# One constant's loads on GpSimd's queue, the identity on the sync queue, and a new order of work

## The chip, the cores and the metric

The kernel runs on one core of one Trainium2 chip. A core has five engines that run their own instruction streams side by side: PE (matrix products; its weight loads are listed apart as PEld), DVE (VectorE), ACT (ScalarE), POOL (GpSimd) and SP (SyncE, which does nothing here but issue transfers). Transfers between DRAM and the core's on-chip memory (SBUF) are moved by 16 DMA engines; each is issued by an instruction of some engine, and an engine issues its transfers in the order in which they stand in its stream. The metric is the device time of one execution in microseconds (us); the median of the runs is compared.

## The reference

Two paths read the same layernormed input and are added to it. Shapes: 2048 tokens, 512 channels, 128 states for each channel, 1792 hidden units; all inputs are bf16.

```python
xn = layernorm(x)                              # over the 512 channels
out = x + A(xn) + B(xn)

# B: gated linear unit
h = sigmoid(xn @ w_gate) * (xn @ w_up)
B = h @ w_down

# A: state-space convolution
logdA = exp(log_dt)[:, None] * (A_re + 1j * A_im)
P = exp(logdA[:, :, None] * arange(2048))                       # 512 x 128 x 2048
K = einsum("dn,dnl,dn->dl", C, P, exp(log_dt)[:, None] * B).real  # 512 x 2048
A = causal_convolution_along_tokens(xn, K) + xn * Dskip         # by FFT of 4096
```

## The kernel before

**The two paths.** The layernorm comes first: four x tiles of 128 tokens by 512 channels are loaded one by one, the others in larger pieces; DVE makes the statistics (L537) and the normalised tiles (L549), and PE transposes the first tiles with an identity matrix (L559, `ident`). Path B then runs in four groups of 512 tokens: gate products (L1042), up products (L1067), ACT's sigmoid (L1055) and copy (L1082), DVE's product of the two (L1087) and the down-projection (L1119). The sum of input and down-projection is made by an accumulating transfer that POOL issues (L1156), 256 KB for two token tiles, in the first three groups.

Path A replaces the long convolution by a transform along the tokens, cut into two steps. The transformed input goes through a DRAM scratch `z_scr`. The convolution kernel K comes from tables of powers that DVE and ACT build (L660 to L740, L789), and PE sums over the states (L820); it goes through a DRAM scratch `k_scr`. Then come 16 *units*: the channels are cut into two halves (p = 0 and 1, of 256 channels), and in each half eight units u = 0 to 7 stand for groups of frequencies. A unit is this chain:

- its input is loaded from `z_scr` (256 KB, on SP), transformed by PE (L881, eight matmuls) and copied to SBUF (ACT, or DVE where `ON_DVE` says so);
- a second copy of it with its halves swapped is made, by four 64 KB transfers on SP (L889) in the first half and for units 4, 6, 7 of the second, and by four DVE copies (L894) for the other five units of the second half;
- its piece of the constant E (`c_E`, 320 KB) is loaded into one of the three slots of the pool `es`, and PE makes the unit's kernel transform from it (L907, ten matmuls);
- DVE multiplies the two (L912, L916), PE transforms back (L931, two matmul shapes), the result is copied and stored to a DRAM scratch `v_scr`.

At the end `v_scr` is read back, and the last PE products (`final`, L1017) add it to what path B left.

**E and its slots.** A slot of `es` is freed by the L907 that reads it. The pieces of units 4, 6 and 7 stay in their slots from the first half to the second (`SHARED`), so there are 8 + 5 = 13 loads; in the second half the loads of units 5, 3, 2, 0 and 1 each wait for a slot that an L907 of this half frees. In the second half the load of unit 5 takes the slot that unit 7's L907 frees, and those of units 0 and 1 the slots of units 5 and 3.

**What sets the order.** `_Plan.add` only records an operation with its engine, its dependences and the slots that it takes and frees. `run` then walks through `ORDER`, a list of all operation numbers, and gives each operation to its engine and each slot to the next taker in that sequence. So `ORDER` sets the stream of every engine, SP's and POOL's too: a transfer whose data or slot isn't there yet holds up all that stands behind it on its engine.

In the lines below, L430 is where every transfer of the helper `dma` is issued (so the profile puts all of them on L430), with the engine as the first argument:

```python
dma("SP", es, cten["E"].ap()[u], deps=w_use[0], acq=[esl], ...)(320 * KB)      # L899
o_held = pl.add("ACT", 0.2, lambda: S.activation(out=ident[:, 127:128], in_=one[:], ...))
l_id = load("ACT", ident[:], cten["ident"].ap(), 32 * KB, deps=[o_held])
```

Before, the identity's transfer is on ACT's queue, behind `o_held`, a small ACT write into a column of `ident`.

Tensors in the profile that are called `big` lie in one large SBUF buffer, so most rows of path A read `big<-big`; `pair` and `bank` are PSUM buffers of 1024 and 512 columns.

Of the kernel before, what the change touches and what calls it, by code (L numbers as in the profile page):

```python
# [13 lines left out]
ACT = mybir.ActivationFunctionType  # L14
# [55 lines left out]
KB = 1024  # L70
# [114 lines left out]
def _consts():  # L185
# [18 lines left out]
                MAB=f(MAB), E=f(_build_E(M2, by).reshape(128, NU // 2, 2, NKT, 128).transpose(1, 0, 2, 3, 4)))  # L204

UEV = (6, 7, 10, 11, 12, 13, 14, 15, 16, 17, 18, 19, 22, 23, 24, 25, 26, 27, 28, 29, 30, 31, 32, 33, 34, 35, 36, 37, 38, 39, 40, 41, 44, 45, 46, 47, 52, 53, 54, 55,)
ON_DVE = (84, 87, 102, 104, 119, 120, 121, 135, 136, 182, 193, 194, 196, 197, 199, 229, 276, 286, 334, 338, 362, 431, 495,)
ORDER = [
# [41 lines left out]

class _Op:
    __slots__ = ("alt", "tab", "eng", "cost", "fn", "prio", "acq", "rel", "dma", "left", "users", "ready", "start", "done", "seq", "mode")
# [69 lines left out]
def kernel(  # L322
# [12 lines left out]
    V, S, T, P, Y = nc.vector, nc.scalar, nc.tensor, nc.gpsimd, nc.sync  # L335
    QUEUE = {"SP": Y, "ACT": S, "POOL": P}
    cten = {k: nc.inline_tensor(v, name="c_" + k) for k, v in _consts().items()}
# [6 lines left out]
    pl = _Plan(dict(s=NS, gu=NGU, hT=NHT, zs=4, zx=2, xx=3, es=3, kb=2, pp=2, pq=2, vs=2, ot=5, tg=2, us=2, sq=2))  # L344
# [14 lines left out]
    ident = const.tile([128, 128], BF, name="ident")  # L359
# [62 lines left out]
    def dma(q, dst, src, deps=(), prio=0.0, acq=(), rel=(), pkt=1024, after=None, hv=0.5):  # L422

        n = None
        get = lambda v: v() if callable(v) else v
        holder = {}

        def fn():
            with nc.allow_non_contiguous_dma(reason="laid out"):
                holder["i"] = QUEUE[q].dma_start(out=get(dst), in_=get(src))  # L430
            if after:
                after(holder["i"])

        return lambda nbytes: pl.add(q, 0.62, fn, deps, prio, acq, rel, dma=(nbytes, _rate(pkt), hv))
# [4 lines left out]
    def load(q, dst, src, nbytes, deps=(), pkt=2048, hv=0.5):  # L439
        lp[0] += 0.01  # L440
        return dma(q, dst, src, deps=deps, prio=lp[0], pkt=pkt, hv=hv)(nbytes)
# [14 lines left out]
    one = const.tile([128, 1], F32, name="one")  # L456
    P.memset(one[:], 1.0)
    S.add_instruction(mybir.InstLoadActFuncSet(name=nc.get_next_instruction_name(), act_func_set_id=LN_EXP_SET))
    o_held = pl.add("ACT", 0.2, lambda: S.activation(out=ident[:, 127:128], in_=one[:], func=ACT.Identity), (), 0)
    l_pa = load("SP", par[:, 0:3, :], A_par[:, 0:3, :], 384 * KB, pkt=3072)  # L460
    l_id = load("ACT", ident[:], cten["ident"].ap(), 32 * KB, deps=[o_held])
    l_pbc = load("SP", par[:, 3:7, :], A_par[:, 3:7, :], 512 * KB, pkt=4096)
    wgv = B_w_gate.rearrange("(kt p) f -> p kt f", p=128)
    wuv = B_w_up.rearrange("(kt p) f -> p kt f", p=128)
# [137 lines left out]
    for n in ["t1", "t2"]:  # L602
# [3 lines left out]
                                                   func=ACT.Exp), [l_pa], 5, tab="exp")  # L606
# [113 lines left out]
    w_use, g_use = [[], []], [[], []]  # L720
# [25 lines left out]
    for c in range(4):  # L746
# [64 lines left out]
        for half_ in range(2):  # L811
            sl = _Slot("s")

            def f_k(half_=half_, sl=sl, G=G, H=H):
                for y in range(8 * half_, 8 * half_ + 8):
                    pk = bank(sl, y // 4 % 2).rearrange("p (q x) -> p q x", q=4)
                    for comp in range(2):
# [18 lines left out]
                        deps=kq_free + W_op + [o_g], prio=PC, pkt=384)(192 * KB))  # L836
# [29 lines left out]
    for p in range(NP):  # L866
        dsl = slice(DW * p, DW * p + DW)
        for u in UNITS[p]:
# [27 lines left out]
            if p and u in SHARED:  # L896
                esl, es, le = held_e[u]
            else:
                le = dma("SP", es, cten["E"].ap()[u], deps=w_use[0], prio=QP - 0.5, acq=[esl], pkt=2560, hv=0.9)(320 * KB)  # L899
                held_e[u] = esl, es, le  # L900
            sk = _Slot("s")

# [306 lines left out]
```

## Time and profile before

| | |
|---|---|
| median of 3 runs | 214.41 us (213.24 to 215.0) |
| the profiled execution: its time, its span | 215.62 us, 213.8 us |
| granted TensorE clock, mean | 0.996 |
| instructions in the span | 4897 |
| moved by DMA | 42.07 MB, 197 GB/s in the mean |
| accumulating transfers on POOL (q0) | 1.57 MB, 5.1% of the 16 engines' span |

How to read what the prediction shows of the profile: the span is the time from the first to the last instruction of one execution; the execution's own time has a little around it. Busy shares are of the span. The slices cut the span in 40 equal parts of 5.34 us, a digit for each: the busy share in tenths. In rows of groups, `xN` is the number of instructions, and the number after the bar the busy time and the mean of one in ns. In rows of the timeline the first number is the start in us, the second the duration of the row, and the brackets give the idle time just ahead and what ended it. A wait `A <- B` stands for idle time of A that B's end finished, as total, count and longest. SPq is the sync queue's own issuing.

### The profile page before, as it was taken

To read this page: it belongs to the slowest core of one execution; us is meant where nothing else is said; L and a number is where in the kernel's file an instruction comes from. 1 tells how busy PE (TensorE), PEld (TensorE's weight loads), DVE (VectorE), ACT (ScalarE), POOL (GpSimd) and SP (SyncE) were. 2 spreads that over 40 slices of the span, in tenths; PEclk is the share of its full clock that TensorE was granted. 3 is DMA by queue.
4 is the path that set the end of the run, shared out by engine and by line. 5 is a ranking of instruction groups with operands and counts; after the bars stand their busy time and mean duration, and the time that the engine had idled before them with its cause. 6 is when DMAs were issued, how large, how long until landed. Compare 5 with 4: busy or idle time off the path is not lost.

```text
span 213.8 us, 4897 instructions
## 1 busy us (share of the span) xinstructions
PE 204.4 (96%) x1856; PEld 102.4 (48%) x1856; DVE 195.5 (91%) x412; ACT 171.5 (80%) x274; POOL 16.8 (8%) x30
## 2 busy tenths in 40 slices
PE   7898999999999999999999999999999979999992
PEld 2653444444444454445437464544653636644571
DVE  3889999999999999999999999999997979994583
ACT  3599999999999999988799998877968777891000
POOL 1003006200820000110000000011000000000000
PEclk9999999999999999999999999999999999999998
DMA  5999379101791457897575778787585569989644
GB/s 169 310 395 364 126 171 311 55 6 38 244 165 46 147 167 249 202 208 189 115 219 143 218 208 251 196 237 156 126 224 161 145 188 321 312 236 296 213 172 172
DMA packets 51465, 42.07 MB, mean 197 GB/s; under 512 B 16545, under 2 KB 44978, under 8 KB 51250
## 3 DMA queue, kind: packets, MB, share of 16 engines
q1 hardware_dynamic: 49650, 39.72, 61.7%
q0 software_dynamic: 864, 1.57, 5.1%
q10 hardware_dynamic: 928, 0.47, 0.8%
q8 instruction: 14, 0.23, 0.4%
q14 instruction: 9, 0.07, 0.1%
HBM read 24.44 MB, written 12.85 MB: 174 GB/s over the span
## 4 chain that ended last, share of the span: by engine, by line
DVE 61%; PE 20%; DMA 6%; ACT 5%; issue 4%; SPq 1%; DVEq 0%; ACTq 0%
DVE big L735 10%; DVE big L734 10%; DVE big L740 5%; DVE big L739 5%; PE bank L1119 4%; DVE hT_sb L1087 4%; PE bank L1042 4%; PE pair L931 3%; DVE big L673 3%; DVE big L675 3%; DVE big L912 3%; PE pair L907 3%; DVE hT_sb L1092 3%; PE bank L1067 3%; DVE stats L537 2%
## 5 line engine op out<-in xcount | busy, mean ns | idle before, releaser
L291 ACT ACTIVATE big<-pair 128x1024 bf16<-128x1024 f32 x62 | 64.3, 1065 | 9.1 <-PE pair L881 1.7
L1067 PE MATMUL bank<-xnT,wu_sb 128*128 128x512 bf16 x224 | 53.6, 379 | 0.1
L1119 PE MATMUL bank<-wd_sb,hT_sb 128*128 128x512 bf16 (+1 forms) x238 | 50.4, 367 | 0.0
L1042 PE MATMUL bank<-xnT,wg_sb 128*128 128x512 bf16 (+1 forms) x200 | 46.8, 371 | 1.0 <-ACT hT_sb L1055 0.9
L1042 PEld LDWEIGHTS <-wg_sb 128*128 128x128 bf16 x240 | 22.4, 98 | 26.1 <-issue 4.7
L1119 PEld LDWEIGHTS <-hT_sb 128*128 128x128 bf16 x238 | 22.5, 98 | 25.0 <-issue 1.6
L1067 PEld LDWEIGHTS <-wu_sb 128*128 128x128 bf16 x224 | 20.9, 98 | 25.0 <-issue 2.9
L1055 ACT ACTIVATE hT_sb<-bank 128x512 bf16<-128x512 f32 x48 | 29.2, 682 | 0.4 <-PE bank L1042 0.4
L734 DVE TENSOR_TENSOR big<-big 128x1024 bf16<-128x1024 bf16 (+4 forms) x40 | 26.7, 668 | 0.1
L1082 ACT ACTIVATE us_sb<-bank 128x512 bf16<-128x512 f32 x40 | 26.0, 680 | 0.9 <-DVE hT_sb L1087 0.7
L735 DVE TENSOR_TENSOR big<-big 128x1024 bf16<-128x1024 bf16 (+4 forms) x40 | 26.6, 665 | 0.0
L907 PE MATMUL pair<-big 128*128 128x256 bf16 x160 | 19.5, 273 | 2.1 <-DMA big<-c_E 1.5
L912 DVE TENSOR_TENSOR big<-big 128x2048 bf16<-128x2048 bf16 x16 | 19.5, 1220 | 1.2 <-DMA big<-big 1.1
L907 PEld LDWEIGHTS <-big 128*128 128x128 bf16 x160 | 15.3, 98 | 6.8 <-DMA big<-c_E 1.8
L789 ACT ACTIVATE sq_sb<-big 128x256 bf16<-128x256 bf16 (+2 forms) x20 | 14.4, 722 | 3.7 <-DVE big L740 3.3
L739 DVE TENSOR_TENSOR big<-big 128x512 bf16<-128x512 bf16 (+4 forms) x40 | 16.5, 412 | 0.1
L740 DVE TENSOR_TENSOR big<-big 128x512 bf16<-128x512 bf16 (+4 forms) x40 | 16.5, 412 | 0.0
L1087 DVE TENSOR_TENSOR hT_sb<-hT_sb,us_sb 128x1024 bf16<-128x1024 bf16 x20 | 13.6, 680 | 0.0
L666 ACT ACTIVATE big<-big 128x1024 f32<-128x1024 f32 x11 | 13.3, 1211 | 0.0
L931 PE MATMUL pair<-big 64*64 64x512 bf16 (+1 forms) x256 | 13.1, 327 | 0.1
L660 ACT ACTIVATE big<-big 128x512 bf16<-128x512 f32 x20 | 12.7, 754 | 0.0
L291 ACT ACTIVATE big<-big 128x256 bf16<-128x256 bf16 x25 | 11.2, 510 | 0.5 <-PE pair L820 0.5
(99 smaller groups left out, 216.8 us busy)
## 6 DMA issues: line engine op xcount, KB each, us to landing
big<-c_E SPq DMA_DIRECT2D x13, 320.0 KB, 4.1
z_scr<-big SPq DMA_DIRECT2D x16, 256.0 KB, 3.5
big<-z_scr SPq DMA_DIRECT2D x16, 256.0 KB, 3.9
v_scr<-big SPq DMA_DIRECT2D x16, 256.0 KB, 3.8
big<-big SPq DMA_DIRECT2D x44, 64.0 KB, 2.7
wu_sb<-in_B_w_up_dram SPq DMA_DIRECT2D x2, 896.0 KB, 9.4
wd_sb<-in_B_w_down_dram SPq DMA_DIRECT2D x1, 1792.0 KB, 9.9
out_dram<-big SPq DMA_DIRECT2D x7, 256.0 KB, 2.2
```

The lines of the kernel that those rows point to most:

```text
L291: nc.scalar.activation(out=get(out), in_=get(in_), func=ACT.Identity)
L734: V.tensor_tensor(out=wide(outp), in0=wide(lo), in1=mre, op=ALU.mult)
L735: V.tensor_tensor(out=wide(tb()), in0=wide(lo), in1=mim, op=ALU.mult)
L739: V.tensor_tensor(out=outp[:, :, 0], in0=outp[:, :, 0], in1=tb()[:, :, 1], op=opr)
L740: V.tensor_tensor(out=outp[:, :, 1], in0=outp[:, :, 1], in1=tb()[:, :, 0], op=opi)
L907: T.matmul(two(sk)[:, o:o + DW], es()[:, g, kt, :], kTv[p][:, :, kt, :], start=kt in (0, NKT - 1), stop=kt >= NKT - 2)
L912: V.tensor_tensor(out=pp().rearrange("p q h m -> p (q h) m"), in0=xx().rearrange("p q h m -> p (q h) m"), in1=kb()[:, 0:2 * DW].unsqueeze( ...
L1042: T.matmul(bank(sl, k % 2)[:, c0:c1], w[:, kt, k * 128:(k + 1) * 128], xnT[:, grp, kt, c0:c1], start=(kt == 0), stop=(kt == KT - 1))
L1055: S.activation(out=hT_sb[:, hs.idx, k % 2, :], in_=bank(sl), func=ACT.Sigmoid)
L1067: T.matmul(bank(sl), wu_sb[:, kt, k * 128:(k + 1) * 128], xnT[:, grp, kt, :], start=(kt == 0), stop=(kt == KT - 1))
L1082: eus.append(pl.add("ACT", 0.48, lambda sl=sl, us=us, kk=kk: S.activation(out=us_sb[:, us.idx, kk % 2, :], in_=bank(sl), func=ACT.Identity ...
L1119: T.matmul(bank(po)[:, 0:c[1] - c[0]], hT_sb[:, hts[k // 2].idx, k % 2, jj * 128:(jj + 1) * 128], wd_sb[:, k, c[0]:c[1]], start=first and ...
```

## The change

It does four things, and computes the same.

1. The 13 loads of E are issued by POOL (GpSimd) instead of SP.
2. The identity is issued by SP instead of ACT, third in SP's stream, behind the x tiles 0 and 1 and ahead of 2 and 3; the ACT write `o_held` is gone. Since it was operation 4, all later operations have a number lower by one.
3. `ON_DVE`, the list of copies that run on DVE, loses five and gains two, in the numbers of before: 276, 334, 338 (small copies of a table's seeds), 431 and 495 (copies of 128 x 1024 from PSUM, one in each half) go from DVE to ACT; 569 and 583 (of the same size, both in the second half) go from ACT to DVE.
4. `ORDER` is a new list, different nearly everywhere.

```diff
-ON_DVE = (84, 87, 102, 104, 119, 120, 121, 135, 136, 182, 193, 194, 196, 197, 199, 229, 276, 286, 334, 338, 362, 431, 495,)
+ON_DVE = (83, 86, 101, 103, 118, 119, 120, 134, 135, 181, 192, 193, 195, 196, 198, 228, 285, 361, 568, 582,)
 ORDER = [
-    0, 1, 2, 3, 5, 4, 6, 16, 13, 8, 12, 15, 7, 22, 25, 27, 26, 28, 29, 35, 30, 31, 37, 32, 24, 36, 38, 39, 34, 40,
...
+    0, 1, 5, 2, 3, 4, 15, 12, 7, 11, 14, 6, 21, 24, 26, 25, 27, 28, 34, 29, 30, 36, 31, 23, 35, 37, 38, 33, 39, 40,
...
-    o_held = pl.add("ACT", 0.2, lambda: S.activation(out=ident[:, 127:128], in_=one[:], func=ACT.Identity), (), 0)
     l_pa = load("SP", par[:, 0:3, :], A_par[:, 0:3, :], 384 * KB, pkt=3072)
-    l_id = load("ACT", ident[:], cten["ident"].ap(), 32 * KB, deps=[o_held])
+    l_id = load("SP", ident[:], cten["ident"].ap(), 32 * KB)
...
-                le = dma("SP", es, cten["E"].ap()[u], deps=w_use[0], prio=QP - 0.5, acq=[esl], pkt=2560, hv=0.9)(320 * KB)
+                le = dma("POOL", es, cten["E"].ap()[u], deps=w_use[0], prio=QP - 0.5, acq=[esl], pkt=2560, hv=0.9)(320 * KB)
```

The lists below show an engine's stream row by row, as source line, operation, written from read tensor and shape; `x3` stands for three alike in a row. Lines of after are higher by one from L430 on.

On SP, the second half's units: `big<-big 32x1024` are the half swaps of 64 KB, `big<-k_scr` is the load of the convolution kernel's table that the second half's L907 read, `v_scr_104<-big` a store of a unit's result. Before:

```order
L430 DMA big<-k_scr 128x4x192
L430 DMA big<-big 32x1024 x3
L430 DMA c_scr<-k_scr 32x1x16
L430 DMA big<-big 32x1024
L430 DMA big<-in_A_u_dram 4x512
L430 DMA v_scr_101<-big 128x4x256 x2
L430 DMA big<-big 32x1024
L430 DMA big<-in_A_u_dram 4x512
L430 DMA big<-c_E 128x1280
L430 DMA big<-big 32x1024 x2
L430 DMA big<-c_E 128x1280
L430 DMA xnT<-v_scr_101 128x2048
```

After:

```order
L431 DMA big<-k_scr 128x4x192
L431 DMA big<-z_scr 128x4x256
L431 DMA big<-big 32x1024 x4
L431 DMA c_scr<-k_scr 32x1x16
L431 DMA v_scr_101<-big 128x4x256
L431 DMA big<-in_A_u_dram 4x512
L431 DMA v_scr_101<-big 128x4x256
L431 DMA big<-big 32x1024 x2
L431 DMA big<-in_A_u_dram 4x512
L431 DMA xnT<-v_scr_101 128x2048
L431 DMA v_scr_104<-big 128x4x256 x2
```

Before, unit 5's piece of E was the first `big<-c_E` here, with ten transfers between the table's load and it, half swaps among them; now no load of E stands on SP, and the swaps follow one another.

On POOL, the end of its stream; `glu_sb` and `big<-in_A_u` are the accumulating transfers of L1156. Before:

```order
L497 TENSOR_SCALAR ln_ve_b<-mvb 128x4
L498 TENSOR_TENSOR ln_sd_b<-ln_ve_b,half 128x4
L768 MEMSET big 128x64x2
L769 MEMSET big 128x64x2
L1156 DMA glu_sb<-in_A_u_dram 128x1024 x4
L1156 DMA big<-in_A_u_dram 128x1024 x2
```

After:

```order
L1156 DMA glu_sb<-in_A_u_dram 128x1024 x2
L768 MEMSET big 128x64x2
L769 MEMSET big 128x64x2
L1156 DMA glu_sb<-in_A_u_dram 128x1024 x2
L431 DMA big<-c_E 128x1280 x7
L1156 DMA big<-in_A_u_dram 128x1024
L431 DMA big<-c_E 128x1280
L1156 DMA big<-in_A_u_dram 128x1024
L431 DMA big<-c_E 128x1280 x5
```

Seven of the first half's loads stand behind the fourth accumulating transfer, the eighth (unit 6) between the fifth and the sixth, and the second half's five are last.

On PE, from unit 7's kernel transform (its last matmul is the first row) to the first matmul of unit 5's (the last row) in the second half, the first row of each group of matmuls. Before:

```order
L907 MATMUL pair_64<-big 128x256
...
L907 MATMUL pair_63<-big 128x256
...
L1067 MATMUL bank_65<-xnT,wu_sb 128x512
...
L881 MATMUL pair_64<-big,m_90 64x512
...
L907 MATMUL pair_63<-big 128x256
...
L931 MATMUL pair_64<-big 64x512
...
L1042 MATMUL bank_66<-xnT,wg_sb 128x512
...
L881 MATMUL pair_63<-big,m_90 64x512
...
L907 MATMUL pair_64<-big 128x256
```

After:

```order
L907 MATMUL pair_63<-big 128x256
...
L907 MATMUL pair_64<-big 128x256
...
L1067 MATMUL bank_66<-xnT,wu_sb 128x512
...
L881 MATMUL pair_63<-big,m_90 64x512
...
L1042 MATMUL bank_67<-xnT,wg_sb 128x512
...
L907 MATMUL pair_63<-big 128x256
...
L931 MATMUL pair_64<-big 64x512
...
L1067 MATMUL bank_66<-xnT,wu_sb 128x512
...
L931 MATMUL pair_63<-big 64x512
...
L907 MATMUL pair_64<-big 128x256
```

Unit 5's transform stands two groups later, one of L1067 and one of L931: behind unit 7's there are now two transforms, two groups of L881 (they follow one another, so one row), two of L1067, one of L1042 and two of L931, where before there were two transforms, two of L881, one each of L1067, L1042 and L931.

81 rows, old and new, of the table ORDER are left out of this document.

## The prediction

> **What bounds the kernel now.** I read the page's busy shares and slices first, then busy time by stage, then the waits, and last the chain of work and the timeline of the one stage with gaps.
>
> ```profile
> span 213.8 us, 4897 instructions
> ...
> PE 204.4 (96%) x1856; PEld 102.4 (48%) x1856; DVE 195.5 (91%) x412; ACT 171.5 (80%) x274; POOL 16.8 (8%) x30
> ...
> PE   7898999999999999999999999999999979999992
> ...
> DVE  3889999999999999999999999999997979994583
> ```
>
> TensorE and VectorE are both at nine tenths nearly everywhere. PE's one dip between the first four slices and the last is slice 33 (171 to 176 us); DVE dips at slices 31 and 33 and at the end. By stage (columns: stretch, its length, then PE, PEld, DVE, ACT and POOL busy, granted clock, DMA share, GB/s):
>
> ```profile
> 20.00:60.00 40.00, 39.99 (x204) 17.56 (x202) 39.72 (x97) 40.00 (x69) 10.52 (x14) 1.00 0.50 147
> 60.00:150.00 90.00, 89.77 (x931) 43.24 (x930) 89.72 (x200) 82.31 (x140) 3.46 (x4) 1.00 0.69 182
> ...
> 165.00:170.00 5.00, 4.44 (x35) 2.80 (x34) 4.43 (x9) 3.99 (x6) 0.00 (x0) 1.00 0.56 149
> 170.00:175.00 5.00, 3.53 (x38) 1.86 (x36) 3.85 (x8) 4.24 (x5) 0.00 (x0) 1.00 0.56 133
> 175.00:190.00 15.00, 14.92 (x159) 8.69 (x158) 14.72 (x21) 11.53 (x15) 0.00 (x0) 1.00 0.99 308
> ```
>
> From 20 to 150 us no order can win more than a few tenths: PE is busy 129.76 of 130 us. From 165 to 175 us PE loses 0.56 + 1.47 = 2.03 us and DVE 0.57 + 1.15 = 1.72 us; then both are full again, so what is lost there is carried to the end. The waits name the causes (total, times, longest):
>
> ```profile
> PEld L907 <- DMA big<-c_E: 1.8, 1, 1.8
> ...
> DVE big L912 <- DMA big<-big: 1.1, 1, 1.1
> ...
> PE pair L559 <- DMA ident<-c_ident: 0.7, 1, 0.7
> ```
>
> Of 13 loads of E one is waited for. The chain from 162 to 176 us shows why that one is late:
>
> ```profile
> 168.49 0.57 SPq L430
> ...
> 169.11 0.63 SPq L430
> ...
> 169.84 4.58 DMA big<-c_E
> ```
>
> The sync queue issues one transfer after the other, 0.57 to 0.63 us each, and E of the second half's unit 5 goes out at 169.84.
>
> **The change, step by step.** *E on GpSimd.* PE at that place before:
>
> ```profile
> 166.15 2.36 PE L907 MATMUL pair<-big 128*128 128x256 bf16 x20 [0.56 <-ACT big L291]
> 168.35 1.03 PE L1067 MATMUL bank<-xnT,wu_sb 128*128 128x512 bf16 x4
> 169.31 0.41 PE L881 MATMUL pair<-big,m 64*64 64x512 bf16 x4
> 169.65 1.27 PE L907 MATMUL pair<-big 128*128 128x256 bf16 x10
> 170.84 0.84 PE L931 MATMUL pair<-big 64*64 64x512 bf16 x16
> 171.62 1.04 PE L1042 MATMUL bank<-xnT,wg_sb 128*128 128x512 bf16 x4
> 172.59 0.41 PE L881 MATMUL pair<-big,m 64*64 64x512 bf16 x4
> 174.47 1.27 PE L907 MATMUL pair<-big 128*128 128x256 bf16 x10 [1.47 <-DMA big<-c_E]
> ```
>
> The load of unit 5 needs the slot that unit 7's L907 frees, the first ten of the twenty that start at 166.15, so about 167.3 us (ten of them, one unit's kernel transform, take half of 168.35 - 166.15, 1.10 us). SP came to it 2.5 us later. GpSimd has only E loads left then, and can issue at 167.3. How long such a load takes is bounded by GpSimd's own transfers, which accumulate 256 KB, and by E's 320 KB on the sync queue (issue in ns and landing in us, minimum, median, maximum):
>
> ```profile
> L1156 POOL DMA_DIRECT2D glu_sb<-in_A_u_dram x4: 866/970/1209, 57.9 to 94.3; - x4
> ...
> DMA to landing us min/median/max: 4.2/5.0/5.5
> ```
>
> ```profile
> L430 SPq DMA_DIRECT2D big<-c_E x13: 320/448/1603, 97.5 to 178.8; - x13
> ...
> DMA to landing us min/median/max: 3.2/4.1/5.4
> ```
>
> I take 5.0 (the same queue), with ends 3.2 and 5.5 + 1.2: it lands at 172.3. Of the work that the new order has between unit 7's transform and unit 5's, the rows above give the size from start to start: two more transforms (1.10 + 1.19), three groups of L1042 and L1067 (0.97 each, from 171.62 to 172.59), two of L881 (0.34) and two of L931 (0.78), together 7.4 us, where before it was 5.7. The transform of unit 5 thus comes up at 174.7, with the load 2.4 us ahead of it; the wait of 1.47 (PE) to 1.8 us (weights) goes, and 1.7 us of work that stood behind it is done instead. I take -1.6. What is late next are units 0 and 1, whose slots the transforms of units 5 and 3 free: PE covers each with two transforms, two L1067 and three L931 groups, 2 x 1.19 + 2 x 0.97 + 3 x 0.78 = 6.7 us, against 5.0.
>
> *Thirteen issues leave SP, thirteen reach POOL.* POOL has room (16.8 us busy; 13 x 0.97 = 12.6 more). Its only waits ahead of an E are two accumulating loads (L1156) in the first half; the E behind the first of them is unit 6's, wanted last of the eight. I cost this at nothing; the cover is that unit 7's transform comes before unit 6's. SP gets 5 x 0.6 = 3 us free between 163 and 179, so the 64 KB swaps are issued earlier; DVE's 1.1 us for one of them is the same stall seen from DVE, and is not counted twice.
>
> *Ident.* It leaves the ACT queue, with the write that held it back, and stands third on SP.
>
> ```profile
> 2.26 4.17 DMA ident<-c_ident
> 6.43 0.14 issue
> 6.57 0.90 PE pair L559 x8
> ```
>
> ```profile
> 4.86 0.66 DVE L537 BATCH_NORM_STATS2 stats<-big 128x6 f32<-128x512 bf16 x1
> 5.60 0.74 DVE L549 TENSOR_SCALAR big<-big,mv,ln_ri_f 128x512 bf16<-128x512 bf16 x2
> ```
>
> The transposes also need the two normalised tiles, made from 5.60 to 6.34, so an earlier ident is worth 0.2 at most, not the 0.7 of the wait. Against it the third x tile is issued one issue later (0.45 us) and behind ident's bytes; its statistics stand on DVE ahead of the normalising at 5.60, with 0.1 us to spare. Bounds -0.2 and +0.6; I take +0.2, since the lost cover is certain and the gain is capped.
>
> *Copies between engines.* Five go from DVE to ACT, two the other way.
>
> ```profile
> L289 DVE COPY big<-big 128x256 bf16<-128x256 bf16 x11 | 2.9, 272 | 0.0
> ...
> L289 DVE CAST big<-pair 128x1024 bf16<-128x1024 f32 x2 | 2.4, 1216 | 1.0 <-PE pair L881 1.0
> ```
>
> DVE loses three small ones and trades two evictions for two: 3 x 0.27 = 0.8 us less, spread over the stretch before the last table, on which the transform at 166.15 depends. PE's 0.56 us of waiting there could go with it, but the tables reach it through DRAM, so I take 0, ends -0.6 and +0.3 (ACT has 7.7 us free from 60 to 150).
>
> *The rest of the order.* Ahead of the last table, between it and the second half's first transform, and behind that, PE has the same groups as before; only their sequence inside these stretches differs. With 0.24 us of gaps in 130, it can win nothing and lose some: 0, ends -0.2 and +1.5 (one wait like the one for E).
>
> **Sum.** -1.6 + 0.2 = -1.4 us. The profiled execution took 215.62 (span 213.8 and 1.8 around it): 214.2. The median of the runs shown is 214.41, 1.2 below it: 213.0. About 1%, 2.1 us, is what a measurement of this kernel can tell from no change.
>
> **Rivals.** *More is won* (211.6): the 0.56 in front of the first transform goes too, the head wins its 0.2 and the load its full 1.8: -0.6 - 0.2 - 1.8 = -2.6, and 0.2 from the scatter of gaps between 20 and 150. For it: DVE lost 1.72 there as well. Against: the tables pass through DRAM whatever the order.
>
> *VectorE holds GpSimd back* (213.5).
>
> ```profile
> L894 DVE COPY big<-big x20: 414/418/423, 163.0 to 185.9; 32x1024 bf16<-32x1024 bf16 x20
> ```
>
> ```profile
> L497 POOL TENSOR_SCALAR ln_ve_b<-mvb x3: 289/567/2411, 17.7 to 53.7; 128x4 bf16<-128x4 bf16 x3
> ```
>
> ```profile
> 142.21 0.87 POOL L1156 DMA_DIRECT2D big<-in_A_u_dram  x1 [47.05 <-DMA big<-z_scr]
> 142.23 1.22 DVE L735 TENSOR_TENSOR big<-big 128x2048 bf16<-128x2048 bf16 x1
> ```
>
> The same small POOL instruction took 0.29 and 2.41 us, so something holds POOL at times. DVE's half copies run in fours, 1.67 us, in just the stage of the last five loads. A load held for four copies and landing slowly takes 5.5 + 1.7 = 7.2: within unit 5's 7.4, but 0.5 past the 6.7 of units 0 and 1. That is -1.6 + 0.5 + 0.2 = -0.9 us, 213.5. Against it, a transfer issued under an addition or product of two tensors, the last two rows, took 0.87 and none of the five others over 1.21. No row of before has one issued under the copies. [...]
>
> *Slower* (216.7): the path from a freed slot to the landed load passes PE's cover. At units 0 and 1 each us beyond 6.7 is PE's; the gain is gone at 8.1 and from 10.2 the kernel is over 1% slower. Two issues in a row as stretched as that worst POOL row and the slowest landing make 2.4 + 2.4 + 5.5 = 10.3, +2.2 us, 216.7. Against: it needs every worst at once, and none of the six transfers of POOL's comes near.
>
> *The order opens a new wait* of 1.5 to 4 us in the full stretch from 20 to 150 (214.5 to 217): every engine's sequence is new there, and three engines are full until 80 us; against it, PE's groups keep their places against DVE's and ACT's within some us. *The load is hidden anyway* (214.4) is out: its row has 1.8 us.
>
> **How the numbers follow.** Forecast, within 1%: 0.36. More is won, faster by over 1%: 0.34. POOL held, within 1%: 0.08. New wait: 0.06 within 1% and 0.08 over it. Path past its cover, slower: 0.08. So faster 0.34, same 0.50, slower 0.16. The likeliest case's own range is 212.3 to 214.4; the 8-in-10 range reaches from 211.2 (all bounds on the gaining side, -1.8 - 0.2 - 0.6 - 0.2 = -2.8, and 0.4 for the scatter of the runs) to 216.2.
>
> **What would show it.** E issued by POOL about 1 us after unit 7's transform ends, each issue near 1 us, landing near 5; no row of L907 waiting for c_E; PE 14.5 us or more of 15 busy from 160 to 175; the first transposes at 6.6 to 7.2 us; and the last token group's down-projection, now at 193.3, about 1.4 us earlier:
>
> ```profile
> 193.30 1.90 PE L1119 MATMUL bank<-wd_sb,hT_sb 128*128 128x512 bf16 x8
> ```
>
> It is wrong if L907 of units 0 or 1 waits for c_E, if an issue on POOL stretches beyond 2 us under L894, or if a PE gap over 1 us stands between 20 and 150 us.

## The result and the profile after

| | before | after |
|---|---|---|
| median (range, runs) | 214.13 us (213.24 to 215.06, 6) | 217.43 us (215.49 to 217.63, 6) |
| ratio, 95% interval | | 1.0122 [1.0084, 1.0159] |
| profiled execution: its time, its span | 215.62, 213.8 us | 217.36, 215.6 us |
| granted TensorE clock, mean | 0.996 | 0.988 |

The changed kernel was slower by 1.2%, where 1.4 us less had been forecast, and above the range. A later comparison on another chip gave it 215.03 us against 214.71, a ratio of 1.0022 [0.9988, 1.0056]; how far that can be explained is part of what follows. (Executions of one kernel lie up to 6 us apart here, 35 of the 46 above 216 us had a mean granted clock of 0.987 to 0.992 and all others that list it 0.995 or more, and the ratios leave out those that are more than 1.5% above the fastest; medians and ranges hold all.)

The page of after, span, busy time and two rows of slices:

```profile
span 215.6 us, 4895 instructions
...
PE 205.6 (95%) x1856; PEld 102.3 (47%) x1856; DVE 195.6 (91%) x409; ACT 172.9 (80%) x276; POOL 25.6 (12%) x43
...
PE   7898999999999699999999999999999999999992
...
DVE  3889999999999977999999999999999999994583
```

The dip of PE in slice 33 (171 to 176 us) is gone, and so are DVE's two at 31 and 33. In their place PE has a dip in slice 14 (70 to 75 us), and DVE in 15 and 16. By stretch, with the same columns as before the change:

```profile
70.00:72.00 2.00, 1.74 (x14) 0.43 (x12) 2.00 (x2) 2.00 (x6) 0.00 (x0) 1.00 1.21 200
72.00:73.60 1.60, 0.00 (x0) 0.00 (x0) 1.60 (x6) 0.98 (x2) 0.00 (x0) 1.00 1.06 323
73.60:75.00 1.40, 1.36 (x4) 0.55 (x5) 1.40 (x5) 0.00 (x0) 0.00 (x0) 0.54 0.65 229
75.00:77.00 2.00, 2.00 (x7) 0.62 (x5) 0.92 (x2) 1.47 (x3) 0.00 (x0) 0.50 0.02 7
77.00:79.00 2.00, 2.00 (x10) 0.94 (x9) 1.76 (x3) 2.00 (x4) 0.00 (x0) 0.97 0.01 4
...
165.00:170.00 5.00, 5.00 (x46) 2.39 (x45) 4.78 (x11) 4.40 (x7) 0.00 (x0) 1.00 0.70 196
170.00:175.00 5.00, 5.00 (x43) 3.00 (x45) 4.76 (x7) 4.38 (x6) 1.11 (x2) 1.00 0.88 255
```

From 165 to 175 PE is now busy 10.00 of 10 us, where it was 7.97: 2.0 us won. From 71.7 to 73.6 it stands still. Then comes something that the profile before had nowhere: the granted clock is 0.54 and 0.50 up to 77 us. PE counts as busy there, but a 128x512 matmul takes 0.63 us in the median instead of 0.38. The timeline of PE shows both:

```profile
70.70 1.04 PE L1067 MATMUL bank<-xnT,wu_sb 128*128 128x512 bf16 x4
73.64 1.86 PE L1042 MATMUL bank<-xnT,wg_sb 128*128 128x512 bf16 x4 [1.90 <-DMA xnT<-x_scr]
75.29 2.80 PE L1067 MATMUL bank<-xnT,wu_sb 128*128 128x512 bf16 x8
77.93 1.03 PE L1042 MATMUL bank<-xnT,wg_sb 128*128 128x512 bf16 x4
```

Four gate matmuls take 1.86 us instead of 1.03, the next eight 2.80 instead of 1.89: 0.83 + 0.91 = 1.7 us more. What they waited for is in the chain of waits:

```profile
61.19 4.13 DMA x_scr<-big
...
65.34 8.25 DMA xnT<-x_scr
...
73.64 1.86 PE bank L1042 x4
```

The third token group's normalised tiles (the expectations count groups from 0 and call it the second) are stored to a scratch (`x_scr`), and a transposing transfer (L578) brings them back as PE needs them. Both are issued by SP. Its stream then and now, before:

```profile
52.94 0.58 SPq L430 DMA_DIRECT2D x_scr<-big  x1
54.49 0.52 SPq L430 DMA_DIRECT2D z_scr<-big  x1
56.52 1.96 SPq L578 DMA_TRANSPOSE xnT<-x_scr  x1
```

and after:

```profile
57.85 2.62 SPq L431 DMA_DIRECT2D z_scr<-big  x4
60.52 0.62 SPq L431 DMA_DIRECT2D m<-c_M  x1
61.19 0.48 SPq L431 DMA_DIRECT2D x_scr<-big  x1
63.94 0.53 SPq L431 DMA_DIRECT2D z_scr<-big  x1
65.34 1.97 SPq L578 DMA_TRANSPOSE xnT<-x_scr  x1
```

Two things make the store go out at 61.19 instead of 52.94. Its last tile is made later: VectorE makes three of the group's four tiles (ScalarE's was done at 44.9 before and at 49.1 after), before in one go and after with the last one at 57.82.

```profile
40.92 1.05 DVE L549 TENSOR_SCALAR big<-big,ln_m_f,ln_ri_f 128x512 bf16<-128x512 bf16 x3
```

```profile
57.82 0.43 DVE L549 TENSOR_SCALAR big<-big,ln_m_f,ln_ri_f 128x512 bf16<-128x512 bf16 x1
```

The store can thus go no sooner than about 58.2, 5 us later than before, and four `z_scr` stores and the load of M ahead of it on SP add the other 3 us. Besides, the transpose takes 8.25 us to land. Before, the answer on line L578 ended with (from issue to landing, minimum, median, maximum):

```profile
DMA to landing us min/median/max: 4.4/4.4/4.5
```

In the profile, 2.0 won for E, 1.9 lost to the transpose and 1.7 to the clock make +1.6 of the +1.8 us between the spans.

### The profile page after: what moved, and what is told of

It is laid out like the page before. It is cut to its first block, busy times and chain, and to the rows that moved or that the text cites. A ratio compares the mean times of both kernels' runs of the same rounds, so it can differ in the third digit from the quotient of the medians.

```text
span 215.6 us, 4895 instructions
## 1 busy us (share of the span) xinstructions
PE 205.6 (95%) x1856; PEld 102.3 (47%) x1856; DVE 195.6 (91%) x409; ACT 172.9 (80%) x276; POOL 25.6 (12%) x43
## 4 chain that ended last, share of the span: by engine, by line
DVE 47%; PE 21%; ACT 12%; DMA 10%; issue 5%; SPq 2%; DVEq 0%; ACTq 0%
DVE big L735 8%; DVE big L734 8%; PE bank L1119 6%; DVE big L740 5%; PE bank L1067 5%; DVE big L739 4%; PE bank L1042 4%; DMA xnT<-x_scr 4%; DMA big<-in_A_u_dram 3%; DVE big L912 3%; DVE big L673 2%; DVE big L675 2%; PE pair L931 2%; DVE hT_sb L1087 2%; DMA x_scr<-big 2%
## 5 line engine op out<-in xcount | busy, mean ns | idle before, releaser
L292 ACT ACTIVATE big<-pair 128x1024 bf16<-128x1024 f32 x62 | 62.7, 1035 | 6.5 <-PE pair L907 1.7
L1067 PE MATMUL bank<-xnT,wu_sb 128*128 128x512 bf16 x224 | 55.1, 384 | 0.0
L1042 PE MATMUL bank<-xnT,wg_sb 128*128 128x512 bf16 (+1 forms) x200 | 48.3, 376 | 3.2 <-DMA xnT<-x_scr 1.9
L1042 PEld LDWEIGHTS <-wg_sb 128*128 128x128 bf16 x240 | 22.5, 98 | 28.6 <-issue 4.2
L1067 PEld LDWEIGHTS <-wu_sb 128*128 128x128 bf16 x224 | 21.3, 99 | 26.5 <-issue 4.5
L1055 ACT ACTIVATE hT_sb<-bank 128x512 bf16<-128x512 f32 x48 | 28.7, 623 | 3.9 <-PE bank L1042 3.8
L1082 ACT ACTIVATE us_sb<-bank 128x512 bf16<-128x512 f32 x40 | 24.3, 627 | 0.7 <-PE bank L1067 0.7
L912 DVE TENSOR_TENSOR big<-big 128x2048 bf16<-128x2048 bf16 x16 | 19.3, 1218 | 0.6 <-ACT big L292 0.6
L907 PE MATMUL pair<-big 128*128 128x256 bf16 x160 | 19.4, 272 | 0.2 <-ACT big L292 0.2
L907 PEld LDWEIGHTS <-big 128*128 128x128 bf16 x160 | 15.5, 98 | 4.4 <-issue 1.1
L789 ACT ACTIVATE sq_sb<-big 128x256 bf16<-128x256 bf16 (+2 forms) x20 | 13.5, 674 | 2.5 <-DVE big L740 2.4
L431 POOL DMA_DIRECT2D big<-c_E x13 | 8.0, 661 | 50.8 <-PE pair L907 43.7
L931 PE MATMUL pair<-big 64*64 64x512 bf16 (+1 forms) x256 | 12.8, 326 | 0.0
L1092 DVE TENSOR_TENSOR hT_sb<-hT_sb,bank 128x512 bf16<-128x512 bf16 x16 | 10.8, 680 | 1.7 <-PE bank L1067 1.3
L666 ACT ACTIVATE big<-big 128x1024 f32<-128x1024 f32 x11 | 12.2, 1106 | 0.1
```

The source lines that it names most:

```text
L292: nc.scalar.activation(out=get(out), in_=get(in_), func=ACT.Identity)
L907: T.matmul(two(sk)[:, o:o + DW], es()[:, g, kt, :], kTv[p][:, :, kt, :], start=kt in (0, NKT - 1), stop=kt >= NKT - 2)
L912: V.tensor_tensor(out=pp().rearrange("p q h m -> p (q h) m"), in0=xx().rearrange("p q h m -> p (q h) m"), in1=kb()[:, 0:2 * DW].unsqueeze( ...
L1042: T.matmul(bank(sl, k % 2)[:, c0:c1], w[:, kt, k * 128:(k + 1) * 128], xnT[:, grp, kt, c0:c1], start=(kt == 0), stop=(kt == KT - 1))
L1055: S.activation(out=hT_sb[:, hs.idx, k % 2, :], in_=bank(sl), func=ACT.Sigmoid)
L1067: T.matmul(bank(sl), wu_sb[:, kt, k * 128:(k + 1) * 128], xnT[:, grp, kt, :], start=(kt == 0), stop=(kt == KT - 1))
```

## The experiments

Each ratio is to the kernel before, run on the same chip with it; its median there is in brackets. "New order" stands for the changed kernel.

**E alone in the old order.**

```diff
-                le = dma("SP", es, cten["E"].ap()[u], ...)
+                le = dma("POOL", es, cten["E"].ap()[u], ...)
```

> The order, the identity and the copies of before, with only the 13 loads of E issued by GpSimd. Theory S (the new order's late transpose costs a stall of 1.9 us and then a halved TensorE clock, and the loads of E on GpSimd are a gain by themselves): L907 no longer waits for E, PE is busy 14.5 us or more of 15 from 160 to 175, the clock stays at 1.00 from 60 to 90, and the time is 1.5 to 2 us under before, about 212.4. Rival G (loads on GpSimd disturb the rest, by their place in its stream or by sharing with VectorE): as slow as the changed kernel, 215 us or more, with waits for E or for the accumulating transfers.

215.16 us [214.09], ratio 1.0047 [1.0018, 1.0075]: rival G's time, but without its waits, and not theory S's gain. PE waits neither for E nor for an accumulating transfer, but the time is no better, if anything worse. VectorE's timeline, and PE's behind it:

```profile
172.44 0.69 DVE L916 TENSOR_TENSOR big<-big 128x1024 bf16<-128x1024 bf16 x1
174.60 1.23 DVE L912 TENSOR_TENSOR big<-big 128x2048 bf16<-128x2048 bf16 x1 [1.46 <-DMA big<-big]
```

```profile
181.20 0.41 PE L931 MATMUL pair<-big 64*64 64x256 bf16 x8 [0.60 <-DVE big L916]
182.33 0.84 PE L931 MATMUL pair<-big 64*64 64x512 bf16 x16 [0.72 <-ACT big L291]
```

VectorE waits 1.46 us for a half swap (a 64 KB transfer of SP), 1.07 before. Full from there on, it hands the loss to PE at L931: 1.3 us, nearly what the wait for E had cost (1.47). A second stall had stood in the shadow of the first.

**The store first, in the new order.** SP's stream:

```diff
+L431 DMA x_scr<-big 128x4x512
 L431 DMA z_scr<-big 256x1x512 x4
 L431 DMA m_90<-c_M 128x1024
-L431 DMA x_scr<-big 128x4x512
-L431 DMA z_scr<-big 256x1x512
 L578 DMA_TRANSPOSE xnT<-x_scr 128x4x512
-L431 DMA z_scr<-big 256x1x512 x5
+L431 DMA z_scr<-big 256x1x512 x6
```

> The changed kernel, with the store of the second group's normalised tiles put ahead of the four z_scr stores and the load of M on the sync queue, and its transpose one place earlier. Theory S: the store goes out at about 58.3 instead of 61.2, the transposed data is there before PE wants it at 71.7, the stall of 1.9 us and the low clock behind it (0.54 and 0.50 from 73.6 to 77, which costs 1.7 us) both go: 3.6 us less than the changed kernel, about 213.8. Rival G: the time stays at 216.5 or more whatever becomes of that stall. Rival C (the low clock has another cause than the stall): only the stall goes, 215.5, with a clock under 0.9 still somewhere from 70 to 90.

213.88 us [214.09], ratio 0.9999 [0.9967, 1.0031]; its span is 212.0, 3.6 us under that of after, as theory S had it. Nothing else was moved, on any engine. In its profile the stall and the low clock are gone (one of the 12 executions, at 217.13 us, has a mean clock of 0.989):

```profile
70.00:75.00 5.00, 5.00 (x30) 2.17 (x26) 5.00 (x12) 5.00 (x11) 0.00 (x0) 1.00 0.60 183
75.00:80.00 5.00, 4.83 (x150) 2.60 (x149) 5.00 (x11) 4.69 (x9) 0.00 (x0) 1.00 0.23 76
```

**E back on SP, in the new order.**

```diff
-                le = dma("POOL", es, cten["E"].ap()[u], ...)
+                le = dma("SP", es, cten["E"].ap()[u], ...)
```

> The changed kernel with the loads of E back on the sync queue, at the places where the order has them. Theory S: the stall for the transpose and the low clock stay, since neither has to do with E, and a wait of up to 1.5 us for E may come back: 217 to 219. Rival G: 215.8 or less.

213.92 us [214.09], ratio 0.9993 [0.9962, 1.0025]: 3 us less than theory S said and in the range of rival G, though its profile (span 213.1) has the very stall that theory S foresaw:

```profile
73.07 1.04 PE L1042 MATMUL bank<-xnT,wg_sb 128*128 128x512 bf16 x4 [1.82 <-DMA xnT<-x_scr]
73.95 1.89 PE L1067 MATMUL bank<-xnT,wu_sb 128*128 128x512 bf16 x8
```

After 1.82 us of waiting the matmuls run at full speed; after 1.90 they ran at half. And 7 of its 12 runs lie under 214 us, so that they can hardly have had the whole stall. E was not waited for, and PE is busy 15.00 of 15 us from 160 to 175, so moving E to GpSimd is no cause of the gain there. That it is no cause of the loss either can't be read from this time. It rests on the stall being here too, on the traces, in which no load of E is issued before 94 us, 20 us behind the stall, and on the same pair without the stall, further down.

**M behind the store, in the new order.** SP's stream:

```diff
 L431 DMA z_scr<-big 256x1x512 x4
+L431 DMA x_scr<-big 128x4x512
 L431 DMA m_90<-c_M 128x1024
-L431 DMA x_scr<-big 128x4x512
```

> The changed kernel with the load of M (0.62 us of issue, 256 KB) behind the store of the normalised tiles instead of ahead of it. Theory S: the store and the transpose go out 0.6 us earlier, the stall shrinks from 1.9 to 1.2 us, under the 1.47 us after which the clock stayed at 1.00 before, so the clock stays up and the gain is 0.7 + 1.7 = 2.4 us: about 215.0. Rival C (the clock drops whatever the stall's length, or for another cause): 0.7 us less only, 216.7, with the clock near 0.5 for some 3 us.

214.55 us [214.09], ratio 0.9996 [0.9963, 1.0030], but three of the 12 executions lie between 217.62 and 219.73, with a mean clock of 0.988 to 0.992. In its profile the transpose landed in 6.5 us and there was no stall at all, so this run doesn't test the length of one.

**The changed kernel and the one before, once more**, on another chip.

> The changed kernel itself once more, for a second look at the stall and for the scatter of its time. Theory S2: the times fall in two heaps about 1.7 us apart, near 215.5 without and 217.4 with the halved clock, most in the upper one, and the profile has the stall for the transposed data near 72 us. Rival G: one heap near 217.4, also where the clock stays up.

215.03 us [214.71], ratio 1.0022 [0.9988, 1.0056]. The profile has no stall at 72 us: the transpose landed in 6.2 us instead of 8.25, with the same streams on all engines. Three of the 12 runs have a mean clock of 0.987 to 0.990, and they are the three above 217 us; the lower ones are spread from 213.7 to 216.2, and the upper heap held 3 of 12, not most.

> The kernel before once more, for a second look at its wait for E. If the wait of 1.47 us is a feature of the kernel, PE loses about 1.5 us again from 170 to 175 and the span is near 213.5. If it is one of two states of its runs (which lie between 213.3 and 215.5), a run near 213.4 has a wait under 0.5 us there.

216.71 us, with a wait of 1.89 us for E: worse than the one of the prediction, and with the low clock behind it. Timeline of PE, and the stretches:

```profile
174.12 1.87 PE L907 MATMUL pair<-big 128*128 128x256 bf16 x10 [1.89 <-DMA big<-c_E]
175.92 1.49 PE L931 MATMUL pair<-big 64*64 64x512 bf16 x16
```

```profile
175.00:177.00 2.00, 2.00 (x21) 0.92 (x19) 1.39 (x2) 0.93 (x1) 0.00 (x0) 0.50 0.86 241
177.00:179.00 2.00, 2.00 (x17) 0.89 (x10) 1.83 (x3) 1.38 (x3) 0.00 (x0) 0.74 1.05 381
```

So the kernel before pays for a halved clock too, in some executions: 7 of its 29 on this chip, from 216.49 to 216.92 us, have a mean clock of 0.988 to 0.992, as this one has 0.992.

**The new order without its stall, E on SP.** Both edits above together.

> The new order with the store of the normalised tiles first, and the loads of E on the sync queue again. Theory S2 (the engine that issues E is worth nothing in the new order; its stall and the low clock behind it are all of the loss): within 0.5 us of 213.9, the time of the same kernel with E on GpSimd, and no row of L907 waiting for E. Rival Q (GpSimd's loads cost some 1.5 us spread over the kernel, which the stall of the run with E on the sync queue hid): about 212.4. Rival W (E is late on the sync queue): 215 or more with a wait for E near 165 to 185 us.

213.56 us [214.71], ratio 0.9972 [0.9946, 0.9999], no wait for E. With E on GpSimd it was 213.88 on another chip (ratio 0.9999 [0.9967, 1.0031]): the two are equal within 0.5 us, as S2 said.

**The identity alone, in the old order.**

```diff
-    o_held = pl.add("ACT", 0.2, lambda: S.activation(out=ident[:, 127:128], ...), (), 0)
...
-    l_id = load("ACT", ident[:], cten["ident"].ap(), 32 * KB, deps=[o_held])
+    l_id = load("SP", ident[:], cten["ident"].ap(), 32 * KB)
```

> Before, with only the identity moved to the sync queue behind the second x tile and the small ACT write left out. Theory S2: the first transposes wait for the normalised tiles instead, the gap ahead of the gate matmuls at 16.8 us takes up what is won, and the time is that of before within 0.4 us, 213.7 to 214.5. Rival H (the identity was late by 0.7 us and that is all carried to the end): 213.4. Rival X (x tiles 2 and 3 come late and hold up VectorE): 214.7.

214.78 us [214.71], ratio 1.0009 [0.9971, 1.0047]: nothing that can be measured. The first transposes start at 5.70 instead of 6.57 us, but so they did where the identity had not been moved (E alone in the old order, 5.70). It had the wait for E as well, 1.81 us, and the clock stayed up.

**GpSimd's accumulating transfers later, in the new order.** The transpose at 65.34 had company: GpSimd issued two accumulating transfers of 256 KB from 65.38 on. First, POOL's stream:

```diff
-L1156 DMA glu_sb<-in_A_u_dram 128x1024 x2
 L768 MEMSET big 128x64x2
 L769 MEMSET big 128x64x2
-L1156 DMA glu_sb<-in_A_u_dram 128x1024 x2
+L1156 DMA glu_sb<-in_A_u_dram 128x1024 x4
```

> The changed kernel with GpSimd's first two accumulating transfers (512 KB together, issued at 65.38 us, in the same moment as the transpose at 65.34) put behind the two zero fills and ahead of the other two, some 20 us later. Theory A (the transpose is slow because the accumulating transfers take the DMA engines with it): it lands in 6 us or less after its issue, PE waits under 0.3 us for it in the profile, no run shows the halved clock, and the time is that of the kernel with the store first, 213.6 to 214.0 where before is near 214.4. Rival Z (the z_scr stores and the load of M ahead of it are what it shares with): it lands in 8 us as before, the wait of 1.8 us and the times of the changed kernel stay.

214.13 us [214.81], ratio 0.9975 [0.9946, 1.0005]; the transpose landed in 6.6 us, and no matmul waited for it (a weight load did, 0.4 us). One of the 12 executions took 218.07 us at a mean clock of 1.0, which no trace explains. And the edit did less than it should: nothing held GpSimd behind the zero fills, and the transfers still went out 0.28 us behind the transpose (65.15 against 64.87; the next expectation's 1.5 us is a misreading). In a second kernel they stand behind the third accumulating transfer, in `ORDER`:

```diff
-    719, 778, 180, 668, 218, 663, 190,
+    719, 778, 180, 218, 190,
...
-    282, 294, 740, 785, 177, 735,
+    282, 294, 740, 668, 663, 785, 177, 735,
```

> The changed kernel with GpSimd's first two accumulating transfers behind the third, which GpSimd cannot issue before some 95 us, so that none of them runs beside the transpose near 65 us. (In the kernel with them behind the zero fills they still went out 1.5 us after the transpose, which landed in 6.6 us; the same kernel unmoved gave 8.3 and 6.2.) Theory A: the transpose lands in 5.5 us or less, as in the old order (4.4 to 4.7), there is no wait for it and no run with the halved clock, 213.7. Rival Z (the z_scr stores and the stretch of DMA work issued at once at 57 us are what it shares with): it lands in 6 us or more, and some of the 12 runs lie above 217.

215.58 us [214.44], ratio 1.0051 [1.0012, 1.0089]. What theory A said of the transpose came out, and PE did not wait for it (line L578):

```profile
DMA to landing us min/median/max: 4.5/4.5/4.5
```

The time did not, for all four accumulating transfers went out from 94.35 on, with three loads of E at 96.8, and a load of `z_scr` at 97.85 ran beside them. Chain of work, and PE:

```profile
97.85 11.15 DMA big<-z_scr
```

```profile
109.04 0.41 PE L881 MATMUL pair<-big,m 64*64 64x512 bf16 x4 [1.97 <-DMA big<-z_scr]
109.38 2.58 PE L1067 MATMUL bank<-xnT,wu_sb 128*128 128x512 bf16 x8
111.75 1.92 PE L1042 MATMUL bank<-xnT,wg_sb 128*128 128x512 bf16 x4
```

That load took 11.15 us, where such loads took 3.9 in the median before and 5.0 after. PE waited 1.97 us, and its clock was halved again (0.50 from 111 to 113 us). The loss had moved by 35 us. Whether the accumulating transfers or the loads of E made this load late, the run doesn't separate.

**The swaps first, in the old order.** If the half swaps are what stands behind E, three small loads (1.9 us of SP's time) can make way for them, and for E too where it is on SP. SP's stream with E on SP; the other kernel has E on POOL besides:

```diff
-L430 DMA big<-big 32x1024 x3
-L430 DMA c_scr<-k_scr 32x1x16
-L430 DMA big<-big 32x1024
-L430 DMA big<-in_A_u_dram 4x512
+L430 DMA big<-big 32x1024 x4
 L430 DMA v_scr_101<-big 128x4x256 x2
 L430 DMA big<-big 32x1024
-L430 DMA big<-in_A_u_dram 4x512
 L430 DMA big<-c_E 128x1280
 L430 DMA big<-big 32x1024 x2
+L430 DMA c_scr<-k_scr 32x1x16
+L430 DMA big<-in_A_u_dram 4x512 x2
```

> The order of before with E on GpSimd, and three small loads (two of 4 KB of x, one of 1 KB of the kernel's scratch, 1.9 us of issue on the sync queue together) put behind the half swaps that VectorE waits for. Theory V (with E out of the way the half swaps are next, and VectorE's wait of 1.46 us for them passes to PE at L931): the swaps land 1.5 to 1.9 us earlier, VectorE's wait and PE's 0.60 and 0.72 us at L931 go, and the time is 1.2 to 1.5 us under that with E on GpSimd alone, about 213.7. Rival D (the swaps are late because the early loads of E fill the DMA engines): no change, 215.

213.69 us [214.81], ratio 0.9974 [0.9944, 1.0004]. VectorE's wait is gone (L912 at 172.99, right behind L916), and the time is 1.5 us under that with E on GpSimd alone (which ran on another chip).

> The same with E left on the sync queue, so that only the three small loads are moved and E of unit 5 is issued 1.9 us earlier too. Theory V: the wait of PE for E (1.47 to 1.9 us in three profiles of this order) and that of VectorE for the swaps both go: 213.4, 1 us under before's median and no run with the halved clock. Rival D: E is not waited for, but the wait for the swaps stays, 214.4.

213.31 us [214.81], ratio 0.9964 [0.9942, 0.9987], and all 12 runs between 213.18 and 213.96. Both waits are gone, with every load of E still on SP:

```profile
165.00:170.00 5.00, 4.96 (x47) 3.43 (x49) 4.86 (x9) 4.30 (x6) 0.00 (x0) 1.00 0.85 228
170.00:175.00 5.00, 4.84 (x56) 2.62 (x50) 4.92 (x9) 4.89 (x6) 0.00 (x0) 1.00 0.58 146
```

Its ratio is the lowest of all that ran, though the intervals of the next ones (0.9972 to 0.9975) overlap with it. It also points to what scattered the kernel before over 213.2 to 217.3 us: the waits at this place, for E and for the swaps, and at times the halved clock behind them.

## Why the prediction was wrong

**The step that failed is the last of the sum, "the rest of the order"**: 0 with an upper end of +1.5, since PE's groups were the same and before had few gaps to win. That looked at what PE does, not at what feeds it. The store and the transpose of a token group are on SP, two queue steps away from any matmul, and it was there that the order changed for the worse: the store later by 8 us, and its transpose issued in the same moment as two accumulating transfers that before followed it by 1.4 us. What the runs showed in place of the 0 is a wait of 1.90 us for the transpose and 1.7 us of halved clock; both went when the store alone was moved. "The order opens a new wait" was among the rivals, with 0.06 + 0.08; it is what happened. Its range of 1.5 to 4 us did hold the 1.9 + 1.7 = 3.6 that removing the stall gave back, but its time (214.5 to 217) was reckoned from 213.0, which the new order did not reach with the stall removed either (213.88).

**A wait was priced at its length.** The upper end was "one wait like the one for E". Here a wait of 1.90 us cost 3.6. Before had a wait of 1.47 without a drop of the clock, so its trace gave no hint.

**E on GpSimd.** The wait went, as forecast, and 2.0 us of gaps with it instead of 1.6. But the cause was named wrongly, so that this part came true by luck: with E back on SP the new order has no wait for E either, and in the old order E on GpSimd wins nothing. The sentence at fault is that VectorE's 1.1 us for a swap "is the same stall seen from DVE, and is not counted twice". It was a stall of its own, and with E gone it took over (1.46 us, handed to PE as 0.60 + 0.72). What did win was the order around it: the three moved loads bring the swaps out earlier (and E, where it is on SP), and in the new order neither is waited for.

**The cost of the loads on GpSimd** was right in kind: an issue took 0.55 us in the median instead of 0.97, landing 5.2 against the assumed 5.0 (up to 7.5), and no L907 waited for it. In the rival in which VectorE's copies hold GpSimd, a load would have been held for up to four copies, 1.7 us. No run shows such a hold: after, the longest issue of the thirteen took 0.89, and of the two under these copies the one at 175.30 took 0.68 and the one at 179.02 0.55, landing in 3.9 and 4.1. So an issue under these copies took at most 0.13 us longer than the median.

**The identity** was put at +0.2 and measured at nothing: the transposes started 0.5 us earlier, at 6.07, and the gap before the gate matmuls at 16.7 us took it up. **The copies between engines** at 0: the 0.56 us of PE before the second half's first transform is gone too, which no run here ascribes to them. **The starting point** was off as well: 1.2 us were taken from the profiled execution to the median, as if the scatter were alike for both kernels, while the wait for E was itself part of what made that execution slow.

**What stays open.** The same streams gave 6.2 and 8.25 us for the transpose. No run was made to find what decides between them, but the traces line up by how far the transpose is issued ahead of the two accumulating transfers (last section). Why the first measurement of after (ratio 1.0122) and the second (1.0022) differ was not found: a profile shows one execution, and of the four in the first that took over 217 us, two have a mean clock of 0.997 and 1.0, so that the halved clock can't be what made them long. That the accumulating transfers are what stretches the transpose is shown by one run (4.5 us without them).

## What to carry to other kernels

When an order is made anew, follow each wait of the bound engine back through the queues that feed it, not only the sequence on the engine itself: the transfers ahead of it in its queue, and those that another queue starts in the same moment. A gap of an engine near full can be two stalls deep, as it was here, so ask what VectorE or the queue waits for once the first is gone, and whether moving a few cheap issues out of the way does more than moving the queue. Gaps on TensorE of 1.89 us and more were dearer here than they are long (1.90 us cost 3.6), and such gaps are worth removing first.

## What the runs showed of the hardware

**The clock dropped after waits of 1.89 us and more, and not after 1.82 and less.** Six profiles have one PE wait of more than a microsecond between 60 and 180 us. After 1.47 (before), 1.81 (the identity alone) and 1.82 us (E back on SP) the matmuls ran on at full clock, granted 1.00; after 1.89 (before once more), 1.90 (after) and 1.97 (the accumulating transfers behind the third) the granted clock was 0.50 for 3.4 us (from 174.6, 73.7 and 110.5), which costs about 1.7 us (0.83 + 0.91 in the timeline of after). It fell 0.5, 0.1 and 1.4 us after PE had started again. What decides between a drop and none was not shown: six waits are too few to tell a fixed limit from chance.

**A transpose issued 0.04 us ahead of GpSimd's accumulating transfers landed in 8.25 us, one 1.42 us ahead of them in 4.4.** Two of 256 KB go out in every profile but one within 3 us of the 512 KB transpose. After, a second profile of after, and before:

```profile
65.38 2.03 POOL L1156 DMA_DIRECT2D glu_sb<-in_A_u_dram  x2
```

```profile
65.08 2.03 POOL L1156 DMA_DIRECT2D glu_sb<-in_A_u_dram  x2
```

```profile
57.94 1.99 POOL L1156 DMA_DIRECT2D glu_sb<-in_A_u_dram  x2 [0.29 <-ACT glu_sb L291]
```

The transpose stands at 65.34, 64.93 and 56.52 there, so it is ahead by 0.04, 0.15 and 1.42 us, and lands in 8.25, 6.2 and 4.4. The other profiles in which its landing can be read fit: 8.2 us with 0.03 ahead, 6.6 and 6.5 with 0.28 and 0.72, and 4.4 to 4.5 with 1.43 to 1.47 in three of the old order. Without them it landed in 4.5. That the lead is the cause was not tested by a run of its own. A 256 KB load beside four of them and three loads of E took 11.15 us, where such loads took 3.9 in the median before and 5.0 after.
